# Rows and components of a spectral layer: which queue issues them, and in how many transfers

## The chip, the cores and the metric

The kernel runs on one core of a Trainium2 chip. The core has four compute engines: TensorE (PE, matrix products, its results in PSUM), VectorE (DVE), ScalarE (ACT) and GpSimd (POOL). A fifth, SyncE (SP), only issues transfers (DMAs). SyncE, ScalarE and GpSimd can each issue transfers, in the order of their own instructions; an instruction that waits holds up what stands behind it on its engine. The metric is the device time of one execution in microseconds, as the median over several runs.

## The reference

The input x has 2048 tokens of 1024 channels, in bf16. Four residual layers follow each other, A, B, A, B, each on the layer-normalised input:

```python
def _layernorm(x, axis=-1, eps=1e-5):
    return (x - mean) / jnp.sqrt(var + eps)

def _A_ref(x, w_r, w_i):                       # spectral layer
    X = rfft2(x, axes=(-2, -1))                # over tokens and channels
    X = X * (w_r + 1j * w_i)                   # filter, 2048 x 513
    return irfft2(X, s=(S, D))

def _B_ref(x, w1, b1, w2):                     # 1024 -> 3584 -> 1024
    h = x @ w1 + b1
    return (h * tanh(softplus(h))) @ w2        # mish

x = x + _A_ref(_layernorm(x), A_w_r, A_w_i)
x = x + _B_ref(_layernorm(x), B_w1, B_b1, B_w2)
x = x + _A_ref(_layernorm(x), A_w_r, A_w_i)
x = x + _B_ref(_layernorm(x), B_w1, B_b1, B_w2)
```

## The kernel before, in words

**Order of work.** The program writes the instructions of every engine out by hand. `Prog` holds one engine's instructions; `op`, `group` and `dma` (L200 to L255) derive the waits from what each instruction reads and writes (`Res`). `dma` places a transfer in the queue of the engine that it is given, at the place that the program has reached for that engine. A `Res` that is written by several transfers as `parts` is ready when all of them have landed.

**The prologue** (L382 to L417). SyncE loads x once by tokens into XS (12 transfers, one more from ScalarE), two small tables, and then x a second time in another order, "rows", into XR: partition 8*n2+h, with the 128 positions n1 and 128 channels l along the free dimension. Each transfer of rows moves one h (of 8) and one quarter q of the n1 positions (32 of 128): 16 x 32 runs of 256 bytes, 128 KB. There are 4 x 8 = 32 of them, on three queues:

- quarters 0 and 2: all eight from SyncE;
- quarter 1: even h from SyncE, odd h from GpSimd, whose issue waits until quarter 0 has landed (`reads=self.r_xr[:1]`);
- quarter 3: even h from SyncE, odd h from ScalarE, issued later (`late_rows`, L413 and L596), after ScalarE's square root in `first_scales`.

Behind the rows SyncE issues FD (the tables of the second stage), JT, the first filter rows (`load_w`, L678), the tables FT and BT and the constants.

**The first stage** (`first_scales`, L586, and `s1`, L626). VectorE and ScalarE compute the layer norm's statistics from XS. A table of scales is transposed on TensorE (L601) and copied (L603). `scaled(j)` (L611) makes the matrices MN for group j from it: on ScalarE for j = 1 (L616, eight small instructions), on GpSimd for j = 2, 4, 9, 10, 11, 13, on VectorE otherwise (L622). Group j of `s1` (16 groups of 8 matmuls, L641) multiplies the rows of positions 8j to 8j+7 with them, so groups 0 to 3 read quarter 0 of XR, 4 to 7 quarter 1, and so on. The result goes to a pair of PSUM banks; three pairs are used in turn here. A copy to Y frees the pair: on ScalarE (L647), on VectorE (L649) for j = 5, 10, 14.

**The other stages** (`order_A`, L1013). Eight groups of components go through s2 (L748, needs Y and FD), s3, the filter (L805 to L837), i1 and i2; `filter_bins` (L1029) prepares a group's filter from rows that were loaded, with four matmuls (L1039) and copies (L1050, L1054). i2 writes group g's components U. `u_turn` (L925) stores them to a scratch tensor in memory, and `u_back` (L949) loads them back in another order into UT, 512 KB in 256-byte runs. Group g's store is followed on SyncE by the load of group g-1. At the end of the layer the order is: i2 of group 6 (copies on ScalarE, L923), `u_turn(6, 1)`, which issues the load of group 5 and then the store of group 6, both from SyncE; then i1 and i2 of group 7, with copies on VectorE (L583) and ScalarE (L579) and its two half stores from ScalarE; `u_back(6)` on SyncE; and `u_last` (L955), four loads of 128 KB for group 7, two from ScalarE and two from SyncE, which wait for both half stores.

**The end of the layer** (L1003 to L1005, L1072). TensorE runs `spin` (4 matmuls, L658), `residual_first` (8, L1067) and `hold` (16 in the first spectral layer, 11 in the second, L663) while the last components travel; then `i4` (L1078) reads UT and the residual is added. The dense layers B follow (L1164), with long streams of matmuls (L1267, L1366).

The second spectral layer (li = 1) takes its rows from layer B through `xn_d` (L545) and `open_xr`, not through the prologue.

Of the kernel before, what the change touches and what calls it, by code (L numbers as in the profile page):

```python
# [7 lines left out]
P = 128  # L8
# [172 lines left out]
class KB:  # L181
# [200 lines left out]
    def prologue(self):  # L382
        sp = self.sp
        self.op(self.pool, lambda e: e.memset(self.EPS[:], 1e-5), writes=[self.r_eps, self.r_warm])
        xt = self.x[0].rearrange("(t p) d -> p t d", p=P)

        for a, b in ((10, 11), (0, 1), (1, 2), (11, 12), (2, 3), (3, 4), (12, 13), (4, 6), (13, 14), (6, 8), (14, 15), (8, 10), (15, 16)):
            self.dma(self.act if a == 10 else sp, self.XS[:, a:b, :], xt[:, a:b, :], f"x{a}", writes=self.r_xs[a:b])
        self.warm(ACT.Sqrt)
        small = {}  # L390
        def load_small(name, n, d):
            b = self.alloc(name, self.o[name], [n], d)
            self.dma(sp, b.ap, self.con[name], name.lower(), writes=[b.res])
            small[name] = b
        load_small("M0", P, BF)
        load_small("IDF", P, F32)
        self.M0, self.IDF = small["M0"], small["IDF"]

        self.XR = self.alloc("XR", self.o["XR"], [P, P])
        self.r_xr = []  # L400
        xv = self.x[0].rearrange("(n2 n1) (h l) -> h n2 n1 l", n2=16, l=P)
        self.r_xr = [Res(f"xr{q}") for q in range(4)]

        def rows(q, h, prog):
            self.dma(prog, self.XR.ap[h:P:8, 32 * q:32 * q + 32, :], xv[h][:, 32 * q:32 * q + 32, :], f"xr{q}{prog.name}",
                     parts=[self.r_xr[q]], reads=self.r_xr[:1] if prog is self.pool else [])
        for q in range(4):
            for h in range(8):
                if h % 2 == 0 or q not in (1, 3):
                    rows(q, h, sp)  # L410
                elif q == 1:
                    rows(q, h, self.pool)
        self.late_rows = lambda: [rows(3, h, self.act) for h in (1, 3, 5, 7)]  # L413
        self.dma(sp, self.FD[:], self.con["FD"], "fd", writes=[self.r_fd])
        load_small("JT", 4 * P, BF)
        self.JT, self.r_jt = small["JT"].ap, small["JT"].res
        self.w1_next = 0  # L417
# [168 lines left out]
    def first_scales(self):  # L586


        dve, act = self.dve, self.act
        for j in range(10):  # L590
            self.stats_dve(j)
        for j in range(10, 16):
            self.stats_act(j)
        self.sums_to_mv(10, 6)
        self.root(0, 16)
        self.late_rows()  # L596
        rt = self.alloc("RT", self.o["RT"], [16, 8], F32)
        self.op(dve, lambda e: e.tensor_copy(rt.ap, self.RS[:, 2, :].unsqueeze(2).to_broadcast([P, 16, 8])),
                reads=self.r_rs, writes=[rt.res])
        bank = self.r_bank[7]  # L600
        self.group([lambda e: e.transpose(self.PS[:, 7, 0:P], rt.ap.rearrange("p a b -> p (a b)"), self.IDF.ap)],  # L601
                   reads=[rt.res, self.IDF.res], writes=[bank])
        self.op(dve, lambda e: e.tensor_copy(rt.ap.rearrange("p a b -> p (a b)"), self.PS[:, 7, 0:P]), reads=[bank], writes=[rt.res])  # L603
        self.MN = self.alloc("MN", self.o["MN"], [P, P])
        self.r_mn = [Res(f"mn{j}") for j in range(16)]
        for r in self.r_mn:
            r.inherit(self.MN.res)
            r.begin()
        self.RT = rt
# [108 lines left out]
    def layer_A(self, li):  # L718
# [7 lines left out]
        dve, act, sp, pool = self.dve, self.act, self.sp, self.pool  # L726
# [198 lines left out]
        def u_turn(g, half):  # L925

            u = U[g % 3]
            if g == 7:
                h = slice(8 * half, 8 * half + 8)
                if half == 0:  # L930
                    u_back(6)
                self.dma(act, self.u_d[g][:, h, :], u.ap[:, h, :], f"uwh{half}", reads=[u.res], writes=[self.r_ud7[half]])
                if half:
                    u_last()
            elif half:
                if g == 6:
                    u_back(5)
                self.dma(sp, self.u_d[g], u.ap, f"uw{g % 3}", reads=[u.res], writes=[self.r_ud[g]])
                if 0 < g < 6:
                    u_back(g - 1)  # L940

# [7 lines left out]
        def u_back(g):  # L949
            if self.UT is None:  # L950
                open_ut()
            self.dma(sp, self.UT.ap[g:P:8, :, :], self.u_d[g].rearrange("l r n -> r l n"), f"usp{g % 3}",
                     reads=[self.r_ud[g]], parts=self.r_ut)

        def u_last():  # L955

            for q in range(4):
                l = slice(32 * q, 32 * q + 32)
                self.dma((act, act, sp, sp)[q], self.UT.ap[7:P:8, l, :], self.u_d[7][l, :, :].rearrange("l r n -> r l n"),
                         f"ul{q}", reads=self.r_ud7, parts=self.r_ut[q:q + 1])  # L960
# [17 lines left out]
        for stage, g, h in self.order_A():  # L978
            if stage == 2:
                s2(g, h)  # L980
                if li == 0 and h == (g < 2):
                    filter_bins(g)
                    if g in (0, 1):
                        load_w(g + 5)
                    elif g == 4:
                        load_w(7)
            elif stage == 3:
                s3(g, h)
                if h:
                    if 1 <= g < 6:  # L990
                        load_tabs(g + 2)
                    if li == 0:
                        self.keep_filter(g)
                    elif g < 4:
                        load_w(g + 4)
            elif stage == 4:
                i1(g, h)
                if h and g < 6:
                    load_btabs(g + 2)
            else:  # L1000
                i2(g, h)
                u_turn(g, h)
# [817 lines left out]
```

## Time and profile before

| what | value |
|---|---|
| median of 6 runs | 928.25 us (925.96 to 930.62) |
| profiled execution | 928.99 us |
| its span, first to last instruction | 927.2 us |
| TensorE busy | 880.7 us (95%) |
| VectorE, ScalarE, GpSimd busy | 623.6, 435.2, 150.0 us |
| transfers | 175.99 MB, mean 190 GB/s |
| first matmul of the first stage (L641) | 22.61 us |
| first matmul of the second stage (L748) | 39.89 us |
| `i4` starts (L1078), first and second spectral layer | 112.70 and 560.85 us |

The profiled execution lies 1.8 us above its span and 0.7 us above the median of the runs. In the timeline a row gives start, duration, engine, line, operation and tiles, how many instructions are merged, and in brackets how long the engine stood idle before it and what ended the wait. An engine's name with a q (SPq, ACTq) is its queue: issuing a transfer, which is not counted as busy. In the chain of work that ended last, each piece is what the next one waited for; "issue" is time for which the profile shows no reason. L251 is the line of the helper `dma`, so all transfers carry it.

### The profile page before, as it was taken

Reading aid. Unit: us, or ns where it says so; the run is one execution under the profiler, and the core shown is the slowest. Engines: PE = TensorE matmul, PEld = TensorE weight load, DVE = VectorE, ACT = ScalarE, POOL = GpSimd, SP = SyncE. Lnnn points to the kernel's source line nnn. Section 1 sums busy time; section 2 is a strip of 40 time slices with the busy share of each in tenths; the row PEclk is TensorE's granted clock in tenths of the full one; section 3 lists DMA queues with packets and bytes.
Section 4 is the critical chain, followed back from the end, with each engine's and each line's share of the span. In section 5 each row is a group of like instructions: output and inputs, shape, how many; then the busy total and the mean of one; then the engine's idle time right before and its main releaser. Section 6 shows DMA issues by size and latency. Waiting matters only on the chain.

```text
span 927.2 us, 13620 instructions
## 1 busy us (share of the span) xinstructions
PE 880.7 (95%) x5503; PEld 473.4 (51%) x5503; DVE 623.6 (67%) x995; ACT 435.2 (47%) x645; POOL 150.0 (16%) x174
## 2 busy tenths in 40 slices
PE   0899989999999999999998998999999999999998
PEld 0677576444444444444446766754444444444443
DVE  7698468687789667568767765666747655554473
ACT  7899485456213485420018975757550015552000
POOL 1732003960004651010121200000000000000000
PEclk9999999999999999999999999999999999999999
DMA  9979872674786388364732786445165545732442
GB/s 275 272 251 273 224 190 67 215 279 120 279 272 240 132 323 292 123 233 142 279 92 104 227 220 152 145 160 173 46 194 189 194 141 191 275 120 83 174 121 110
DMA packets 151711, 175.99 MB, mean 190 GB/s; under 512 B 73080, under 2 KB 130648, under 8 KB 151528
## 3 DMA queue, kind: packets, MB, share of 16 engines
q1 hardware_dynamic: 136160, 129.27, 45.1%
q0 software_dynamic: 10224, 43.42, 12.8%
q10 hardware_dynamic: 5264, 2.43, 1.1%
q8 instruction: 43, 0.70, 0.3%
q14 instruction: 20, 0.16, 0.1%
HBM read 130.78 MB, written 40.89 MB: 185 GB/s over the span
## 4 chain that ended last, share of the span: by engine, by line
PE 87%; DVE 6%; ACT 5%; DMA 1%; issue 1%; ACTq 0%; SPq 0%; DVEq 0%
PE PS L1366 37%; PE PS L1267 30%; PE PS L1227 6%; PE PS L748 3%; PE PS L849 2%; ACT ARENA L457 2%; PE PS L879 2%; PE PS L1078 2%; PE PS L641 1%; PE PS L1188 1%; PE PS L911 1%; PE PS L1067 1%; PE PS L663 1%; ACT ARENA L647 1%; DVE ARENA L1193 1%
## 5 line engine op out<-in xcount | busy, mean ns | idle before, releaser
L1366 PE MATMUL PS<-ARENA 128*128 128x512 bf16 x1568 | 340.1, 379 | 0.0
L1267 PE MATMUL PS<-ARENA 128*128 128x512 bf16 (+1 forms) x1288 | 280.3, 379 | 0.8 <-DVE ARENA L1272 0.8
L1366 PEld LDWEIGHTS PS<-ARENA 128*128 128x128 bf16 x1568 | 153.3, 98 | 184.5
L1272 DVE TENSOR_TENSOR ARENA<-PS,ARENA 128x512 f32<-128x512 f32 x230 | 157.1, 691 | 100.0 <-PE PS L1267 92.2
L1267 PEld LDWEIGHTS PS<-ARENA 128*128 128x128 bf16 x1288 | 125.4, 98 | 153.2 <-DVE ARENA L1272 3.5
L1277 ACT ACTIVATE ARENA<-ARENA,B 128x512 bf16<-128x512 f32 x138 | 98.8, 721 | 69.1 <-DVE ARENA L1272 63.7
L579 ACT ACTIVATE ARENA<-PS 128x512 f32<-128x512 f32 (+3 forms) x86 | 61.6, 726 | 110.8 <-PE PS L1267 92.4
L1160 POOL TENSOR_TENSOR ARENA<-ARENA 128x512 bf16<-128x512 bf16 x56 | 71.4, 1275 | 74.7 <-DVE ARENA L528 61.1
L457 ACT ACTIVATE ARENA<-XS 128x1024 bf16<-128x1024 bf16 x60 | 63.2, 1053 | 36.4 <-DVE XS L1417 33.1
L1227 PE MATMUL PS<-ARENA 128*128 128x256 bf16 (+1 forms) x528 | 74.8, 299 | 3.4 <-DVE ARENA L1193 1.9
L1391 DVE TENSOR_TENSOR ARENA<-ARENA 128x3584 bf16<-128x3584 bf16 x32 | 63.9, 2017 | 0.0
L1227 PEld LDWEIGHTS PS<-ARENA 128*128 128x128 bf16 x528 | 50.8, 99 | 22.9 <-DVE ARENA L1193 3.3
L1417 DVE TENSOR_TENSOR XS<-PS,ARENA 128x512 bf16<-128x512 f32 x52 | 35.7, 690 | 39.0 <-PE PS L1366 38.7
L1409 DVE TENSOR_TENSOR ARENA<-PS,ARENA 128x512 f32<-128x512 f32 x48 | 32.9, 688 | 27.7 <-PE PS L1366 27.3
L1231 ACT ACTIVATE ARENA<-PS,B 128x256 bf16<-128x256 f32 (+1 forms) x66 | 33.2, 515 | 30.2 <-PE PS L1227 30.0
L1277 ACT ACTIVATE ARENA<-PS,B 128x512 bf16<-128x512 f32 x46 | 31.5, 685 | 18.4 <-PE PS L1267 18.4
L1405 DVE TENSOR_TENSOR ARENA<-ARENA,XS 128x512 f32<-128x512 f32 x52 | 36.9, 734 | 0.6
L448 ACT ACTIVATE RS<-MV,EPS 128x1 f32<-128x1 f32 (+2 forms) x11 | 3.3, 296 | 71.6 <-DVE MV L570 70.1
L748 PE MATMUL PS<-FD,ARENA 128*128 128x256 bf16 (+1 forms) x256 | 31.4, 271 | 2.5 <-ACT ARENA L647 1.3
L849 PE MATMUL PS<-ARENA 128*128 128x256 bf16 x256 | 32.6, 273 | 1.0 <-DVE ARENA L814 0.6
L805 ACT ACTIVATE ARENA<-PS 128x1024 bf16<-128x1024 f32 x30 | 30.4, 1046 | 5.0 <-PE PS L796 5.0
L1242 DVE TENSOR_TENSOR ARENA<-ARENA 128x2048 f16<-128x2048 bf16 x16 | 25.3, 1582 | 9.0 <-PE PS L1227 8.7
(103 smaller groups left out, 817.7 us busy)
## 6 DMA issues: line engine op xcount, KB each, us to landing
ARENA<-in_B_w_dram SPq DMA_DIRECT2D x30, 896.0 KB, 6.7
ARENA<-w1s_scratch SPq DMA_DIRECT2D x28, 896.0 KB, 4.8
ARENA<-w2s_scratch SPq DMA_DIRECT2D x24, 896.0 KB, 6.4
w1s_scratch<-ARENA POOLq DMA_DIRECT2D x14, 896.0 KB, 4.5
ARENA<-in_B_w_dram SPq DMA_DIRECT2D x24, 512.0 KB, 4.4
u_scratch<-ARENA SPq DMA_DIRECT2D x14, 512.0 KB, 4.7
ARENA<-u_scratch SPq DMA_DIRECT2D x14, 512.0 KB, 5.8
w2s_scratch<-ARENA POOLq DMA_DIRECT2D x8, 896.0 KB, 4.2
```

What stands on the lines that cost most here:

```text
L457: self.op(act, lambda e, i=i, f=f: e.activation(junk.ap, x, f, accum_out=sums[:, i:i + 1]), reads=[self.r_xs[j]], writes=[junk.res], parts ...
L579: fn = (lambda e: e.activation(dst, src, ACT.Copy)) if scale is None else \
L748: fns.append(lambda e: e.matmul(dst, at(r), FD[:, t:t + n], start=start, stop=stop))
L849: fns.append(lambda e, c=c, part=part: e.matmul(ps[:, c * 256:(c + 1) * 256], yk.ap[:, part, c * P:(c + 1) * P], t[:, (128, 0)[part]:(384, ...
L1160: self.op(self.pool, lambda e, dst=A(dst), x=A(x), y=A(y), op=op: e.tensor_tensor(dst, x, y, op), reads=[b.res] + list(after), writes=[b.rs])
L1227: fns.append(lambda e, db=db, bank=bank, fl=fl: e.matmul(PS[:, bank, 0:w], wb.ap[:, db, fl * P:(fl + 1) * P], x.ap[:, db, tok], start=(db ...
L1267: self.group([lambda e, db=db: e.matmul(PS[:, bank, :], A[:, db, :], mov[:, db, :], start=(start and db == 0), stop=(db == 3), skip_group_ ...
L1272: self.op(dve, lambda e: e.tensor_tensor(dst.ap, PS[:, bank, :], x.ap, ALU.add), reads=[self.r_bank[bank], x.res], writes=[dst.res])
L1277: self.op(act, lambda e: e.activation(at, src, ACT.Mish, bias=self.B1[:, ft:ft + 1]), reads=[res, self.r_b1], writes=[ra])
L1366: self.group([lambda e, i=i, k=k, b=PB[n][k].ap: e.matmul(PS[:, bank, :], ap[:, i, t * P:(t + 1) * P], b[:, i - 7 * k, :], start=(start an ...
L1391: self.op(dve, lambda e: e.tensor_tensor(ap[dst][:, f, :], ap[x][:, f, :], ap[y][:, f, :], op), reads=part(x, k) + part(y, k), writes=part ...
L1405: self.op(dve, lambda e: e.tensor_tensor(a[t], a[t], x, ALU.add), reads=[rx], writes=[r[t]])
```

## The change

Two edits.

1. The rows are loaded in 24 transfers, all from SyncE: quarters 0 and 1 together in eight transfers of 256 KB, which share one `Res`, then quarters 2 and 3 in eight each of 128 KB. GpSimd and ScalarE issue none; `late_rows` and its call go.
2. `u_turn` issues the store of group 6's components from ScalarE's queue, not SyncE's, in both spectral layers. The load of group 5, ahead of it in the program, stays with SyncE.

```diff
@@ prologue
-        self.r_xr = [Res(f"xr{q}") for q in range(4)]
-
-        def rows(q, h, prog):
-            self.dma(prog, self.XR.ap[h:P:8, 32 * q:32 * q + 32, :], xv[h][:, 32 * q:32 * q + 32, :], f"xr{q}{prog.name}",
-                     parts=[self.r_xr[q]], reads=self.r_xr[:1] if prog is self.pool else [])
-        for q in range(4):
+        for q, n in ((0, 2), (2, 1), (3, 1)):
+            r = Res(f"xr{q}")
             for h in range(8):
-                if h % 2 == 0 or q not in (1, 3):
-                    rows(q, h, sp)
-                elif q == 1:
-                    rows(q, h, self.pool)
-        self.late_rows = lambda: [rows(3, h, self.act) for h in (1, 3, 5, 7)]
+                s = slice(32 * q, 32 * (q + n))
+                self.dma(sp, self.XR.ap[h:P:8, s, :], xv[h][:, s, :], f"xr{q}", parts=[r])
+            self.r_xr += [r] * n
@@ first_scales
         self.root(0, 16)
-        self.late_rows()
@@ u_turn
                 if g == 6:
                     u_back(5)
-                self.dma(sp, self.u_d[g], u.ap, f"uw{g % 3}", reads=[u.res], writes=[self.r_ud[g]])
+                self.dma(act if g == 6 else sp, self.u_d[g], u.ap, f"uw{g % 3}", reads=[u.res], writes=[self.r_ud[g]])
```

## The prediction

> **What bounds the kernel now.** I read the chain that ended last first, then its pieces in order of time around both edited places, then the timeline, the row transfers and the busy time by stretch. Over the whole span of 927.2 us the chain is TensorE:
>
> ```profile
> PE 87%; DVE 6%; ACT 5%; DMA 1%; issue 1%; ACTq 0%; SPq 0%; DVEq 0%
> ```
>
> So what the edits touch is a small part, and each matters only where the chain leaves TensorE's steady stream. The first place is the prologue. Its pieces (start us, us, what):
>
> ```profile
> 19.86 0.36 ACTq L251
> ...
> 21.61 0.65 ACTq L251
> ...
> 22.36 2.45 ACT ARENA L616 x8
> 24.82 0.05 issue
> 24.86 2.74 PE PS L641 x24
> 27.60 0.95 issue
> 28.55 5.99 PE PS L641 x56
> ...
> 34.57 1.23 DVE ARENA L649
> 35.80 2.26 DVE ARENA L622 x2
> 38.06 1.14 DVE ARENA L649
> 39.20 0.69 issue
> 39.89 1.69 PE PS L748 x16
> ```
>
> ScalarE's four row issues (L251) stand on the chain ahead of the scaled matrices of group 1 (L616); groups 1 to 3 of the first stage follow (L641). Then comes a hole of 0.95 us with no engine named. Group 4 starts there, the first that reads the second quarter of the rows; half of that quarter is issued by GpSimd. The second stage begins at 39.89 when the copy of group 15 is done (38.77 plus 1.02 us on ScalarE). The timeline (start, us, engine):
>
> ```profile
> 8.11 22.82 SPq L251 DMA_DIRECT2D ARENA<-in_A_x_dram  x24
> ...
> 19.57 2.66 POOL L251 DMA_DIRECT2D ARENA<-in_A_x_dram  x4 [18.72 <-DMA ARENA<-in_A_x_dram]
> ```
>
> GpSimd waits for the first quarter, so that quarter has landed at 19.57. Its own four issues start at 19.57 to 21.61; the median of them lands 5.7 us after its start, so the last at 27.3 or, with the delay of a loaded queue, later: I read the hole's end at 28.5 as this landing. The issue times by transfer (ns min/median/max), rows and then the components' loads, which have the same 256-byte runs but four times the bytes (512 KB against 128 KB):
>
> ```profile
> L251 SPq DMA_DIRECT2D ARENA<-in_A_x_dram x24: 627/628/3087, 8.1 to 30.3; - x24
> ...
> L251 SPq DMA_DIRECT2D ARENA<-u_scratch x9: 532/538/1640, 68.1 to 109.8; - x9
> ```
>
> An issue costs 0.53 to 0.63 us whatever its size, when the queue has room. The stretches (us, PE, PEld, DVE, ACT, POOL, clock, DMA share, GB/s):
>
> ```profile
> 15.00:21.00 6.00, 0.48 (x1) 0.18 (x1) 4.23 (x13) 4.06 (x9) 1.43 (x3) 1.00 0.97 198
> 21.00:28.00 7.00, 3.75 (x32) 3.25 (x32) 6.95 (x7) 5.42 (x12) 6.90 (x7) 1.00 1.15 232
> 28.00:32.00 4.00, 3.44 (x33) 3.48 (x34) 1.66 (x3) 2.50 (x3) 4.00 (x3) 1.00 1.23 217
> ```
>
> From 15 to 21 us one 131 KB issue every 0.67 us gives 195 GB/s: SyncE's pace, not the engines'. With a backlog the rows reach 232 (three queues) or 217 GB/s (SyncE almost alone).
>
> The second place is the end of each spectral layer. In the first layer:
>
> ```profile
> 100.03 0.60 ACT L579 ACTIVATE ARENA<-PS 128x512 bf16<-128x512 f32 x1
> ...
> 100.23 1.45 SPq L251 DMA_DIRECT2D u_scratch<-ARENA  x1
> ...
> 101.23 0.60 ACT L579 ACTIVATE ARENA<-PS 128x512 bf16<-128x512 f32 x1 [0.60 <-PE PS L849]
> ...
> 109.06 3.66 PE L663 MATMUL PS<-BD,ARENA 128*128 128x512 bf16 x16
> ...
> 112.70 0.95 PE L1078 MATMUL PS<-MT,ARENA 128*128 128x32 bf16 x32
> ```
>
> TensorE fills the wait for the components with 16 filler matmuls (L663, 16 x 216 ns, so to 112.5), and the reads start at 112.70.
>
> **The Trainium skill.** "DMA: Bandwidth & Descriptors", section Issuing engines are not separate DMA queues: transfers of all issuers run on the same 16 DMA engines, and several issuers save issue time alone. The trace agrees in kind: three queues give 232 GB/s, one with a backlog 217. The same page, Queues, rings and completion order: the engines alternate between queues packet by packet; so GpSimd's and ScalarE's rows share bandwidth with SyncE's third quarter from 21 us. "TensorE: Matmul & The Clock Gate", Part 1: the array runs at half clock until one free-running window of about 3.4 us is busy, so a hole can delay the full clock. In the trace, first-stage matmuls start 107 ns apart to 34.2 us and 55 ns apart after it, 5.6 us after the hole.
>
> **The change, part by part.**
>
> *SyncE's rows.* 8 + 4 + 8 + 4 = 24 issues become 8 + 8 + 8 = 24; eight carry 256 KB. By the loads of 512 KB the larger ones cost no more to issue (0.63 us), so 24 x 0.63 stays; what waits behind them (FD, JT, the first filter rows) is held by the same 4 MB, and I move it by 0 to 0.7 us. The fourth issue's 3.09 us shows a full queue; larger transfers meet it sooner, but it then has work.
>
> *When the first half lands.* The first quarter is at 19.57 now. The second follows it directly, 1.05 MB: at 198 GB/s 5.3 us, so 24.9; at 217, 4.8 us, and the first gains 0.3, so 24.1; at 232, 23.6; at the 280 GB/s of the stretch 95 to 97 us, 22.4. The larger transfers lift the issue limit; I take 24.0 and keep 22.4 to 24.9.
>
> *ScalarE.* Four issues go, 2.71 us. Its 8 scaled copies wait for VectorE's scales, which end at 21.34, so they start at 21.4, not 22.36, and end at 23.85. *GpSimd.* Four issues go, 2.66 us; its scaled matrices start about 0.95 us earlier and gate nothing.
>
> *The first stage.* Group 0 now waits for both quarters, 24.0, not 22.61: late by 1.4, on nobody's path, as group 1 stands at 24.86. The groups then run back to back at 8 x 107 = 0.853 us: group 4 starts at 24.0 + 4 x 0.853 = 27.4, not 28.55: 1.15 us gained. ScalarE's copies, one per 0.93 us, keep the three PSUM pairs free: copy 0 ends at 26.2, group 3 asks for its pair at 26.6. Group 8 asks for the third quarter near 31 and group 12 for the fourth near 34; at 217 GB/s they land at 28.9 and 33.8. VectorE's steps behind group 10 (1.23 + 2.26 us) shift along. Without the hole the full clock can come up to 3 us sooner; the copies (0.93 against 0.44 us per group) then set the pace, which is worth 0 to 0.7 us; I take 0.3. The second stage starts near 38.4. A cap stands behind it: the filter matmuls at 41.42 need filter rows that land at 39.4 (VectorE waits for them there), so at most 2.0 us pass through. Sum of this part: -1.45 us, bounds -2.0 and, at 24.9, -0.25.
>
> *Group 6's store.* SyncE's 1.45 us issue goes; it stood behind the load of group 5's components. ScalarE gets one issue in each layer, right after the copy that ends at 100.08: 0.33 us by its own stores of group 7 at 103.73, plus 0.05 for the wait. Queued behind it is the copy at 100.03 (0.60 us), now about 100.5 to 101.1; the next starts at 101.23, waiting for TensorE. Cost 0, with 0.13 us in hand; a stall as long as SyncE's 1.45 would cost 1.0 us per layer, but ScalarE's queue is empty then. The store no longer waits behind the 512 KB load and lands up to 2 us sooner; SyncE's next load (105.45) follows. What gains: in layer 0 the reads start 0.2 us after the fillers; in layer 1 directly behind them. So -0.2 and 0; against it, the earlier load runs beside group 7's stores and could delay the last loads by up to 0.5 us where they are just in time. I take -0.1.
>
> **Sum.** -1.45 - 0.1 = -1.55 us on the span of 927.2, so 925.65. The profiled execution took 928.99 (1.8 us outside the span) and becomes 927.45. The median of the runs is 928.25; the same difference gives 926.7. About 0.3% (2.8 us) is the least that a measurement of this kernel can tell from no change, so this counts as none.
>
> **Rivals.** *Capped (B):* the filter rows land 0.7 us later and take the prologue's gain. For it: VectorE waits for them at 39.41. Against: their wait is 0.21 us, and the same bytes stand ahead of them. It gives 927.6 to 928.6.
>
> *Late rows (C), the slower side:* a 256 KB transfer needs twice the room in the queue, SyncE issues the next only when half has drained, and the engines run dry in between. For it: the stalls of 3.09 and 2.15 us. Against: with 512 KB loads queued the engines kept 231 GB/s from 99 to 103 us. At worst each transfer waits for the one ahead: 262 KB in 1.21 us (217 GB/s) plus 0.63 us of issue, 143 GB/s. I allow 1.4 us from last byte to landing (half of the 2.8 us that the shortest row transfer takes in all); then 3.2 us x 198 GB/s = 0.63 MB of the first quarter were left at 15 us, and with the second 1.68 MB. At 143 GB/s they take 11.7 us, the half is there at 28.1, group 4 starts at 31.5, 3.0 us late, and the kernel takes 931.2. The rival decides from 25.15 us on (24.0 plus 1.15, about 200 GB/s); below 145 GB/s it is slower by over 0.3%.
>
> *More (D):* rows at 280 GB/s; group 1 is then bound by ScalarE's 23.85, group 4 starts at 26.4 (-2.1), and with the full clock early and filter rows moved along the gain is 2.3 to 3.3: 925 to 926.
>
> **Chances.** A (-0.7 to -2.3) 0.50, B 0.17, C 0.19, D 0.14. A and B lie within 0.3%; of C I give 0.11 past it, as its rate is unbounded below, and of D 0.09. So faster 0.09, same 0.80, slower 0.11. The range, 924.4 to 930.4, covers A, B, most of D and the milder half of C, with some 0.7 us for the median of six runs (925.96 to 930.62); what is left out is 0.12 above and 0.06 below. A alone has 925.9 to 927.6.
>
> **What would show it.** In the changed profile: SyncE's first eight row issues at about 0.63 us with stalls; no row issue on ScalarE or GpSimd; the first L641 group near 24.0 and no hole before the fifth; L616 from 21.4; L748 near 38.4; L641's 55 ns spacing before 34.2. At the layers' ends: ScalarE's store near 100.1 at 0.33 us, the copy behind TensorE still 0.60 after its matmul, the load of group 6 sooner, L1078 directly behind L663. The forecast is wrong if the first L641 group starts after 25.2, if L748 follows FD or filter rows, or if L1078 stands behind its loads.

## The result, and the profile after

The changed kernel takes 929.94 us (median of 16 runs, 928.27 to 934.75); the kernel before, in all its runs beside it, 927.57 (37 runs). The ratio is 1.0029 with an interval of 1.0018 to 1.0039: slower by 2.7 us (1.7 to 3.6), close to the 0.3% that the prediction took as the least that can be told from no change. It had put the median at 926.7 us and counted that as no change. The profiled executions agree: a span of 929.1 us against 927.2. Below, layer 1 and layer 2 are the first and the second spectral layer.

The chain of waits over the whole span of the changed kernel:

```profile
PE 83%; DVE 6%; DMA 4%; ACT 4%; SPq 2%; issue 1%; ACTq 0%; DVEq 0%
```

Where TensorE held 87% and transfers 1%, TensorE now holds 83% and transfers 4%. The chain therefore leaves TensorE in more places. Its pieces in the prologue (start us, us, what):

```profile
20.07 5.13 DMA ARENA<-in_A_x_dram
...
25.24 1.05 PE PS L634 x8
...
26.31 6.53 ACT ARENA L640 x7
...
38.89 1.69 PE PS L741 x16
40.58 0.45 PE PS L1032 x4
```

The first-stage group (L634, L641 before) waits for the last row transfer of the first half and starts at 25.24. The hole ahead of the fifth group is gone, ScalarE's copies (L640) set the pace, and the second stage (L741) starts at 38.89, 1.0 us sooner than in the profile of before. The stretches over the row loads (us, PE, PEld, DVE, ACT, POOL, clock, DMA share, GB/s) show how fast they came:

```profile
15.00:21.00 6.00, 0.48 (x1) 0.18 (x1) 4.37 (x14) 3.86 (x9) 0.00 (x0) 1.00 1.12 205
21.00:28.00 7.00, 2.76 (x27) 2.76 (x28) 6.93 (x7) 4.13 (x10) 6.77 (x4) 1.00 1.13 215
```

205 GB/s, not much above the 198 of before: larger transfers did not open a faster rate. The ends of the two spectral layers, in the same chain:

```profile
103.79 5.24 DMA u_scratch<-ARENA
...
554.23 4.88 DMA u_scratch<-ARENA
...
559.18 3.13 DMA ARENA<-u_scratch
...
562.45 0.95 PE PS L1071 x32
```

Here the time is lost. In the second layer of before no transfer stood here; the reads (L1078 then, L1071 now) followed the fillers without a gap:

```profile
558.64 2.37 PE PS L663 x11
561.01 0.79 PE PS L1078 x32
```

Now the reads wait for a store of 4.88 us and a load of 3.13 behind it. TensorE's waits in the changed kernel, from 550 to 566 us (idle us, times, longest):

```profile
PE PS L1071 <- DMA ARENA<-u_scratch: 1.4, 1, 1.4
```

From the first filler behind the last components (L651 now, L658 before) to the first read, layer 1 takes 8.69 us (7.91 before) and layer 2 8.21 (6.68). These +0.78 and +1.54 us and some 0.6 lost in the stretches between and after, less the 1.0 gained in the prologue, make up the 1.9 us between the spans.

The store that now lasts 4.88 us is the second half of group 7's components. It issues where it did, and in the kernel before landed 2.12 us after its issue, by the same view:

```profile
DMA to landing us min/median/max: 2.1/2.1/2.1
```

What changed around it is the order of issues. The timeline of before (start, us, engine):

```profile
553.11 0.33 ACTq L251 DMA_DIRECT2D u_scratch<-ARENA  x1
554.17 0.33 ACTq L251 DMA_DIRECT2D u_scratch<-ARENA  x1
555.06 0.53 SPq L251 DMA_DIRECT2D ARENA<-u_scratch  x1
```

and of the changed kernel:

```profile
553.17 0.33 ACTq L251 DMA_DIRECT2D u_scratch<-ARENA  x1
553.41 0.53 SPq L251 DMA_DIRECT2D ARENA<-u_scratch  x1
554.23 0.33 ACTq L251 DMA_DIRECT2D u_scratch<-ARENA  x1
```

SyncE's load of group 6 (512 KB in runs of 256 bytes) waits for the store of group 6. That store lands sooner, so the load goes out at 553.41, ahead of group 7's last store and not behind it. The records of the transfers' packets say the same: the store's first packet moves 2.8 us after its issue (within 0.9 before). From 555.9 to 557.0 us the changed kernel moves packets of SyncE's queue (q1) alone, and none of ScalarE's, whose store was issued at 554.23 (packets, MB, their time as a share of 16 engines' time, each packet counted in full):

```profile
q1 hardware_dynamic: 1156, 0.30, 129.1%
```

About three quarters of the load's packets have started when the store's begin. The four loads of group 7 (`u_last`) wait for it, and the reads for them.

### The profile page after: what moved, and what is told of

Same layout as the page of the kernel before. It is cut to its first block, busy times and chain, and to the rows that moved or that the text cites. A ratio compares the mean times of both kernels' runs of the same rounds, so it can differ in the third digit from the quotient of the medians.

```text
span 929.1 us, 13610 instructions
## 1 busy us (share of the span) xinstructions
PE 878.4 (95%) x5503; PEld 470.7 (51%) x5503; DVE 623.8 (67%) x995; ACT 435.2 (47%) x645; POOL 147.6 (16%) x170
## 4 chain that ended last, share of the span: by engine, by line
PE 83%; DVE 6%; DMA 4%; ACT 4%; SPq 2%; issue 1%; ACTq 0%; DVEq 0%
PE PS L1359 35%; PE PS L1260 30%; PE PS L1220 6%; PE PS L741 3%; PE PS L842 2%; SPq L251 2%; PE PS L872 2%; PE PS L1071 2%; ACT ARENA L640 1%; DMA ARENA<-in_B_w_dram 1%; DMA u_scratch<-ARENA 1%; PE PS L1181 1%; ACT ARENA L451 1%; ACT ARENA L573 1%; DMA ARENA<-u_scratch 1%
## 5 line engine op out<-in xcount | busy, mean ns | idle before, releaser
L1224 ACT ACTIVATE ARENA<-PS,B 128x256 bf16<-128x256 f32 (+1 forms) x66 | 33.2, 515 | 30.3 <-PE PS L1220 30.0
L1270 ACT ACTIVATE ARENA<-PS,B 128x512 bf16<-128x512 f32 x46 | 31.5, 685 | 18.4 <-PE PS L1260 18.4
L741 PE MATMUL PS<-FD,ARENA 128*128 128x256 bf16 (+1 forms) x256 | 31.4, 271 | 2.5 <-ACT ARENA L640 1.3
```

The costliest lines, as they stand in the source:

```text
L741: fns.append(lambda e: e.matmul(dst, at(r), FD[:, t:t + n], start=start, stop=stop))
L1270: self.op(act, lambda e: e.activation(at, src, ACT.Mish, bias=self.B1[:, ft:ft + 1]), reads=[res, self.r_b1], writes=[ra])
```

## The experiments

The theory is that the loss is the store's edit, through the early load ahead of group 7's last store. Against it stand two others: that the loss comes from ScalarE's queue, which carries one more store, or that it comes from the rows' edit and the layers' ends only pass it on. A second question is why the prologue's gain doesn't reach the time. Times are medians, of 14 to 22 runs where an interval is given; a ratio is to the kernel before on the same chips.

**Each edit alone.** The rows' edit alone:

```diff
-                self.dma(act if g == 6 else sp, self.u_d[g], u.ap, f"uw{g % 3}", reads=[u.res], writes=[self.r_ud[g]])
+                self.dma(sp, self.u_d[g], u.ap, f"uw{g % 3}", reads=[u.res], writes=[self.r_ud[g]])
```

> The rows' edit alone; group 6's store stays with SyncE. Both theories on the layers' ends (load ahead, shared queue; see the next run) put the loss in the store's edit: the second stage then starts near 38.9 us as in the changed kernel (39.89 before), both layers' ends are as before (i4 about 0.2 us behind the fillers in the first layer, directly behind them in the second), and the time is 1.0 us under the kernel before (0.9989). If the rows cost the time, for instance through what follows them in SyncE's queue, it is over the kernel before by up to 2.5 us.

The kernel before with the store's edit alone:

```diff
-                self.dma(sp, self.u_d[g], u.ap, f"uw{g % 3}", reads=[u.res], writes=[self.r_ud[g]])
+                self.dma(act if g == 6 else sp, self.u_d[g], u.ap, f"uw{g % 3}", reads=[u.res], writes=[self.r_ud[g]])
```

> The store's edit alone; rows as before. Theory load ahead: SyncE, free of the store, issues the load of group 6 about 2 us sooner, ahead of group 7's second half store, and this store lands about 5 us after its issue (2.1 in the second layer before). Theory shared queue: group 6's store stands in ScalarE's queue ahead of group 7's. Both expect i4 0.8 to 1.0 us later in the first layer and 1.5 us later in the second, so 2.3 to 3.5 us over the kernel before (1.0025 to 1.004). If the store's edit costs nothing, the time is that of before.

Rows alone: 928.15 us, ratio 1.0009 (0.9995 to 1.0023), span 927.1. Store alone: 930.37, 1.0029 (1.0019 to 1.0040), span 928.9. The store's edit carries the whole loss; the rows' edit makes no difference that can be told, and the gain of 1.0 us expected of it is missing. The chain of the store alone, end of layer 2 (start us, us, what):

```profile
554.29 4.76 DMA u_scratch<-ARENA
...
559.12 3.35 DMA ARENA<-u_scratch
...
562.61 0.95 PE PS L1078 x32
```

The store of 4.76 us and the load behind it stand there as in the changed kernel, without any change of the rows.

**The same order from SyncE, ScalarE's queue untouched.** In the kernel before, SyncE issues the store of group 6 ahead of the load of group 5:

```diff
+                self.dma(sp, self.u_d[g], u.ap, f"uw{g % 3}", reads=[u.res], writes=[self.r_ud[g]])
                 if g == 6:
                     u_back(5)
-                self.dma(sp, self.u_d[g], u.ap, f"uw{g % 3}", reads=[u.res], writes=[self.r_ud[g]])
```

> The kernel before with two transfers of SyncE exchanged at the end of each spectral layer: group 6's store is issued ahead of the load of group 5, not behind it. ScalarE's queue is as before. The store lands about 2 us sooner and so the load of group 6 starts sooner, near 103.4 us. Theory load ahead: group 7's second half store lands about 5 us after its issue and the time is 2 to 3.5 us over the kernel before. Theory shared queue: nothing of ScalarE's has changed, so the time is that of before within 0.5 us.

931.17 us, ratio 1.0036 (1.0026 to 1.0046). Its timeline and then its chain:

```profile
553.82 0.53 SPq L251 DMA_DIRECT2D ARENA<-u_scratch  x1
...
555.08 0.33 ACTq L251 DMA_DIRECT2D u_scratch<-ARENA  x1
```

```profile
555.08 5.38 DMA u_scratch<-ARENA
...
560.53 3.24 DMA ARENA<-u_scratch
...
563.91 0.95 PE PS L1078 x32
```

The load of group 6 again goes out ahead of the last store, which lands after 5.38 us. ScalarE issues here exactly what it did before, so that theory falls: what matters is when group 6's store lands and what it releases.

**The load put back behind the store.** Two kernels keep both edits and move only the load of group 6. In the first, SyncE issues it once all of group 7's components are written:

```diff
@@ u_turn, g == 7
-                if half == 0:
-                    u_back(6)
...
                 if half:
+                    u_back(6, sp, [u.res])
                     u_last()
@@
-        def u_back(g):
+        def u_back(g, prog=sp, after=()):
...
-            self.dma(sp, self.UT.ap[g:P:8, :, :], self.u_d[g].rearrange("l r n -> r l n"), f"usp{g % 3}",
-                     reads=[self.r_ud[g]], parts=self.r_ut)
+            self.dma(prog, self.UT.ap[g:P:8, :, :], self.u_d[g].rearrange("l r n -> r l n"), f"usp{g % 3 if prog is sp else 'a'}",
+                     reads=[self.r_ud[g]] + list(after), parts=self.r_ut)
```

> The changed kernel, with one wait more: SyncE issues the load of group 6 when group 7's components are all written, so at about the moment of group 7's second half store, not 0.4 to 0.8 us before it. Group 6's store stays in ScalarE's queue. Theory load ahead: that half store lands 2.1 to 3.5 us after its issue, i4 stands directly behind the fillers in both layers, and the time is 3 us under the changed kernel, 1.0 under the kernel before. Theory shared queue: the half store lands as late as in the changed kernel, near 5 us, and the time stays near 930.

In the second, the added line is `u_back(6, act)`, directly behind group 7's last store on ScalarE:

> The changed kernel, with the load of group 6 issued by ScalarE right behind group 7's second half store, so 0.35 us after it and in the same queue. Theory load ahead: the half store lands 2.1 to 2.5 us after its issue in the second layer (4.88 in the changed kernel), the last loads start by 556.5, i4 is directly behind the fillers, 6.7 us after the first of them (8.21 in the changed kernel), and the time is 2 to 3 us under the changed kernel. If group 6's store in the same queue were what counts, the half store would still need near 5 us.

927.86 us, ratio 1.0005 (0.9992 to 1.0017), and 927.95 us, 1.0001 (0.9990 to 1.0013): the loss is gone in both. The timeline of the second and its chain:

```profile
552.17 0.33 ACTq L251 DMA_DIRECT2D u_scratch<-ARENA  x1
...
552.53 0.59 ACTq L251 DMA_DIRECT2D ARENA<-u_scratch  x1
```

```profile
552.17 2.60 DMA u_scratch<-ARENA
...
554.84 4.25 DMA ARENA<-u_scratch
...
559.22 0.95 PE PS L1070 x32
```

With the load 0.36 us behind it the store lands after 2.60 us. The last loads now stand behind the load of group 6 and take 4.25 us, not 3.13, but store and loads together are 1.2 us shorter (6.9 against 8.1), and the reads start 7.05 us after the first filler (8.21). In the first of the two the load is issued 0.02 us ahead of the store, the store lands after 2.77 us, and the reads start after 7.32. So the harm comes somewhere between 0.02 us ahead and the changed kernel's 0.82.

Over all profiles of the study the split is clean. Where the load of group 6 goes out ahead (changed kernel twice, store alone, SyncE's order), layer 2's last store takes 4.76 to 5.38 us and the reads start 8.21 to 8.84 us after the fillers; in the thirteen others without an added load 2.02 to 2.83 and 6.45 to 7.72. In layer 1 the reads start after 8.51 to 9.99 us against 7.56 to 8.43, so the groups nearly touch. The store itself is less clear there: 4.94 to 6.23 us with the load ahead, but 2.37 to 4.68 with it behind, 4.37 in the kernel before; what holds it up in those isn't known. Against the medians of the thirteen the changed kernel's two profiles lose 0.75 and 1.5 us at the two ends, which is most of its 2.7.

**Bytes or small runs?** The load ahead moves 512 KB in runs of 256 bytes. To ask which of the two delays the store, the last load stays behind the store on ScalarE, and a further load of the same 512 KB, in 128 runs of 4 KB, goes out early from SyncE. It fills the buffer that the components came from, which nothing reads afterwards; it adds that one transfer per layer.

```diff
@@ u_turn, g == 7, with u_back(6, act) behind the last store
+                if half == 0:
+                    self.dma(sp, U[0].ap, self.u_d[6], "ucoarse", reads=[self.r_ud[6]], writes=[U[0].res])
```

> The changed kernel with the load of group 6 behind the last half store (as in the run before that did so), and at its early place on SyncE another load of the same 512 KB, in 128 runs of 4 KB into group 6's own buffer. It adds 512 KB of loads in each layer. If bytes ahead hold up the store, its second half lands 1.4 us later than with no load there (2.60 us from issue to landing in the second layer), so at 3.5 to 4.2 us. If it is the number of 256-byte pieces ahead, it lands at 2.6 to 3.0 us.

The timeline of this kernel has the extra load 1.03 us ahead of the last store:

```profile
555.48 0.33 SPq L251 DMA_DIRECT2D ARENA<-u_scratch  x1
...
556.51 0.33 ACTq L251 DMA_DIRECT2D u_scratch<-ARENA  x1
```

A single run took 931.24 us. In layer 2 the store landed after 3.82 us, between 2.60 and 4.88; in layer 1 after 6.19, against 4.48 without the extra load and 5.24 in the changed kernel. So 512 KB in long runs ahead delay the store too: in layer 2 by about half as much as small runs do, in layer 1 by more. Small runs are not needed for the delay, and what they add is not settled by one run. An estimate: at the 231 GB/s that the kernel before moved from 99 to 103 us, with such loads queued, 512 KB take 2.3 us, and 2.60 + 2.3 = 4.9 is what the store took in the changed kernel's layer 2. That the store simply stands behind all that was issued ahead of it fits. Whether it waits at the transfer engines or already where the two queues' transfers are cut into packets stays open.

A third kernel sent the load of group 6 from GpSimd, at its old place, to see whether another issuer takes the delay away:

```diff
                 if half == 0:
-                    u_back(6)
+                    u_back(6, pool)
```

> The changed kernel, with the load of group 6 issued by GpSimd in place of SyncE, at the same early place. It separates two ways in which the load can hold up the store. If its bytes do it (the engines are shared), the half store in the second layer still lands near 5 us after its issue and the time is as in the changed kernel, near 930. If it is that SyncE's 2048 descriptors go through what makes ScalarE's descriptors too, GpSimd's own descriptors stay out of the way: the store's packets start about 0.9 us after its issue, it lands in 2.1 to 3.5 us, and the time is 1.5 to 2.5 us under the changed kernel.

928.44 us, 1.0001 (0.9983 to 1.0018), and the last store landed after 2.83 us. But this doesn't tell the theories apart. The timeline has the issue ahead of the store (552.30):

```profile
551.57 1.08 POOL L251 DMA_DIRECT2D ARENA<-u_scratch  x1 [21.19 <-DMA u_scratch<-ARENA]
```

while the load's first packets move at 554.23 only, when nine tenths of the packets of group 7's two half stores have started. GpSimd's load was late enough to restore the order by itself.

**Why the prologue's gain isn't seen.** The prediction took the hole of 0.95 us and the late full clock from one profile. Here are two more profiles of the kernel before and one of the changed kernel, both unchanged:

> The kernel before, unchanged, profiled once more. Theory clock: the hole ahead of group 4 (0.95 us) and the clock that came up only at 34.3 us belong to the one execution that was profiled, not to the kernel; here the clock comes up at 27.5 to 31.5, the first filter matmul starts at 39.4 to 39.9 us, not at 41.42. Theory hole: the hole and the late start are the kernel's own, 28.5 and 41.4 again.

> The same once more, with the same two forecasts: first filter matmul at 39.4 to 39.9 us (clock) or at 41.4 (hole).

> The changed kernel, unchanged, profiled once more. By the other five profiles with its rows the first filter matmul starts at 39.9 to 40.5 us, and the second half store of group 7 lands 4.5 to 5.5 us after its issue in both layers, with i4 8.2 to 9.2 us behind the first filler.

The chains of before, first and second repeat:

```profile
27.88 0.94 issue
28.82 5.57 PE PS L641 x56
...
39.73 1.69 PE PS L748 x16
```

```profile
31.10 1.07 PE PS L641 x16
...
38.17 1.69 PE PS L748 x16
```

These runs took 927.24, 928.16 and, for the changed kernel, 930.3 us. The first repeat has the hole and a second stage at 39.7, as in the profile shown ahead of the prediction; the second has a hole of 0.3 us only, and its second stage starts 1.6 us sooner. With the two kernels that keep the rows of before, its prologue has been seen five times: first filter matmul at 41.42, 41.27, 39.70, 39.47 and 39.87 us. The prediction had one of the two late ones.

In all five, group 4 starts 0.1 us after the last of GpSimd's rows lands (28.46 and 28.55 in the profile of before), so the hole was read rightly. But the hole alone doesn't make a prologue late. In the kernel with SyncE's order (start us, us, engine; idle time in brackets):

```profile
28.51 1.50 PE L641 MATMUL PS<-ARENA 128*128 128x128 bf16 x24 [0.96 <-issue]
```

Here the matmuls behind the hole start 55 ns apart at once, and the second stage starts at 38.30. The late start goes with the full clock: it comes at 34.3 and 33.7 us in the two late profiles and at 28.5 to 29.7 in the three others. In five profiles this is a correlation; no run here shows it as the cause.

With all rows on SyncE in 256 KB transfers seven profiles give 39.87 to 41.44 us for the first filter matmul, median 40.39, against a median of 39.87. The latest is the changed kernel's repeat, forecast at 39.9 to 40.5: its second stage itself waits for FD, to 38.90, and from 39.5 runs at half clock. The two sets overlap; by the medians the rows' edit loses some 0.5 us in the prologue, and a gain of 1.45 isn't there. The place is in the chain of the rows' edit alone:

```profile
24.45 6.11 PE PS L634 x56
...
33.62 6.79 DMA ARENA<-in_A_w_i_dram
...
40.46 0.63 PE PS L1032 x4
```

The first stage runs without a hole, but the first filter matmuls (L1032) now wait for filter rows that SyncE issues at 33.6. In the five profiles with the old rows they start 1.53 to 1.57 us behind the second stage, with nothing between; with the new rows 1.53 to 2.54, median 1.96. One queue for all rows issues FD, and what follows it, later: at 31.7 to 32.5, against 30.3 to 31.5, 0.9 us by the medians.

Two kernels were to test the other half of the reading, the clock, by holding it up. Matmuls that nobody reads run through the two waits of the prologue, in the kernel before (12 at the second place) and in the rows' edit alone (40 there):

```diff
+        def fill(n):
+            self.group([lambda e: e.matmul(self.PS[:, 6, 0:P], self.M0.ap, self.M0.ap, start=True, stop=True)] * n,
+                       reads=[self.M0.res], writes=[self.r_bank[6]])
+        fill(50)
...
+        fill(12)
```

> The kernel before, with TensorE kept busy by matmuls whose result nobody reads: 50 before the table of scales is transposed and 12 behind it, so that the clock is up when the first stage begins. Theory clock: where the second stage starts with the rows of before (39.89, 37.94 and 38.30 us in three profiles) hangs on the moment at which the array's clock comes up (34.3, 29.2 and 28.5 us), so here it starts at 37.5 to 38.0 us, and the median is 0.5 to 1.0 us under the kernel before. Theory rows: the start is set by the GpSimd and ScalarE issues and stays at 38 to 40 us.

> The rows' edit alone, with 50 and 40 such matmuls, so that the clock is up until the first half has landed (24.5 to 25.2 us). Theory clock: with it up in both kernels the rows' edit is worth nothing; the groups run at 0.93 us each, by the copies, from 24.5 on, group 4 starts at 27.5 to 28.0 and the second stage at 37.5 to 38.3, within 0.4 us of the kernel before with the clock up. Theory rows: the edit gains the 1.0 us of the two first profiles here too, so the second stage starts 1 us ahead of the other kernel with the clock up.

926.65 us, ratio 0.9992 (0.9976 to 1.0007), and 928.38 us, 1.0008 (0.9996 to 1.0021). No gain can be told. But the first doesn't test what it was meant to, as the clock was not held. The stretch from the end of group 0 has a granted clock of 0.50 (us, PE, PEld, DVE, ACT, POOL, clock, DMA share, GB/s):

```profile
22.90:29.60 6.70, 4.78 (x47) 4.70 (x46) 5.17 (x6) 6.48 (x12) 6.70 (x5) 0.50 1.25 227
```

The full clock is back at 29.6 us, and the second stage starts at 38.00, like the three early profiles without such matmuls. In the second kernel the clock holds to 34.7 us, and still the second stage starts at 39.44, not at 37.5 to 38.3. Its chain:

```profile
24.93 9.28 ACT ARENA L645 x10
...
34.38 7.24 DMA ARENA<-in_A_w_i_dram
...
41.66 0.63 PE PS L1037 x4
```

The first stage reaches group 12 before its rows (it goes on at 34.71, at half clock to 38.1), and the filter rows land at 41.6, 2.2 us after the second stage has started. In this profile the filter rows set when the filter matmuls start, whatever the clock did ahead of them.

Does the size of the transfers matter? All rows on SyncE in 32 pieces of 128 KB, with the same waits:

```diff
-                s = slice(32 * q, 32 * (q + n))
-                self.dma(sp, self.XR.ap[h:P:8, s, :], xv[h][:, s, :], f"xr{q}", parts=[r])
+                for k in range(q, q + n):
+                    s = slice(32 * k, 32 * k + 32)
+                    self.dma(sp, self.XR.ap[h:P:8, s, :], xv[h][:, s, :], f"xr{q}", parts=[r])
```

> The rows' edit alone with all 32 pieces of 128 KB from SyncE, same waits: the size of the transfers by itself. If SyncE's issue time sets the pace (0.67 us for 131 KB, 195 GB/s), the first half lands at 25 to 26 us (24.3 to 25.2 with 256 KB) and FD goes out about 3 us later, near 35; if the transfer engines do, both are as with 256 KB.

A single run took 929.44 us. The first half lands at 24.58 (24.1 to 25.2 with 256 KB): the size of the transfers did not set its landing. FD goes out at 32.78 and the first filter matmul starts at 42.01, the latest of all; one profile doesn't say whether that is the pieces' doing.

If late filter rows take the gain, giving ScalarE back its four late row transfers should return it. The rows' edit alone, but the odd transfers of the last quarter issued as before:

```diff
+                if q < 3 or h % 2 == 0:
+                    self.dma(sp, self.XR.ap[h:P:8, s, :], xv[h][:, s, :], f"xr{q}", parts=[r])
...
+        self.late_rows = lambda: [self.dma(self.act, self.XR.ap[h:P:8, 96:128, :], xv[h][:, 96:128, :], "xr3a", parts=[r])
+                                  for h in (1, 3, 5, 7)]
@@ first_scales, behind self.root(0, 16)
+        self.late_rows()
```

> The rows' edit alone, with one part of it undone: the odd h of the last quarter again from ScalarE behind its square root. SyncE issues 20 row transfers, not 24. Theory tail of SyncE's queue: in the rows' edit FD goes out at 31.7 to 32.6 us (30.1 to 31.1 with the rows of before), the filter rows behind it arrive later, and the first filter matmul waits for them at about 40.4; here FD goes out at 29 to 30, that matmul starts at 39.3 to 39.7, and the time is 0.5 to 1 us under the rows' edit. If the first stage itself (group 0 at 24.5 us) sets it, the matmul stays at 40.4 and the time at 928.

> The rows' edit with the odd h of the last quarter from ScalarE, once more, to see whether it beats the kernel before. By its first measurement 0.9989 of it, 1 us; if the pair of measurements together does not hold it clear of 1, it is not told from the kernel before.

And the same with the 50 and 40 matmuls that nobody reads:

> The same with TensorE kept busy by 50 and 40 matmuls that nobody reads, so that the clock is up. Theory tail: with neither the clock nor the filter rows late, group 4 starts near 27.0 as in the rows' edit with the clock up, the first filter matmul at 38.5 to 39.3, and the time is 1 us under the kernel before (0.999). The groups' copies at 0.93 us each allow no more than that. If it stays at 40 us or above, something else in the row order holds it.

The first kernel: 926.39 us, 0.9989 (0.9975 to 1.0003), and in the second measurement 927.39, 0.9996 (0.9982 to 1.0011). In its two profiles FD goes out at 30.61 and 30.40 us (forecast 29 to 30) and the first filter matmul starts at 40.02 and 39.72 (forecast 39.3 to 39.7), 1.53 us behind the second stage in both. So the wait for filter rows is gone, as the theory has it; but two of the seven profiles with all rows on SyncE show 1.53 as well, and the time isn't told from that of the kernel before.

With the added matmuls: 927.34, 0.9996 (0.9985 to 1.0007). The first filter matmul starts at 40.74, not at 38.5 to 39.3. The clock is up through the first stage, but it falls again at 37.7, and the second stage's first 16 matmuls, 1.69 us elsewhere, take 3.15 in the chain:

```profile
37.80 3.15 PE PS L750 x16
```

No kernel of the study beats the kernel before with any certainty.

## Why the prediction was wrong, point by point

*Group 6's store* is the step that failed. It named the mechanism in one clause ("the earlier load runs beside group 7's stores and could delay the last loads by up to 0.5 us"), gave it a bound without a working, and took -0.1 us. The measured cost is 2.7 us in the times, of the changed kernel (1.7 to 3.6) and of the store's edit alone (1.8 to 3.7), and +0.78 and +1.54 us at the two layers' ends in the profiles. Two things were missed. First, the order: SyncE's load was put down to the first layer's 105.45, "sooner", without asking where it lands against ScalarE's last store. In the second layer of before that store was issued 0.89 us ahead of the load, and a release 2 us sooner must turn the two around. Second, the size: by the prediction's own 231 GB/s a load of 512 KB takes some 2.3 us, an estimate that would have been a bound; the store lost 2.8 us in layer 2, of which the reads felt 1.5. That the reads stood directly behind the fillers was seen (in layer 1 too, where the 0.2 us taken as a gap is the end of the last filler in the view), and it meant that there was next to no slack; it was used to say that nothing could be gained, not that all that is late is lost. What the step said of ScalarE was right: the issue takes 0.33 us (99.12), the copy behind it goes out at 99.50, and the next still starts 0.02 us after its matmul, at 100.24.

*SyncE's rows.* The count was right, the pace wasn't. 24 issues of 0.63 us were kept, but SyncE was held up: on the chain the issues ahead of the last row transfer of the first half take 3.62, 1.44, 1.15, 1.17 and 1.06 us. FD was moved by "0 to 0.7 us"; it went from 30.97 to 32.47, 1.5 us.

*When the first half lands.* Forecast 24.0 (22.4 to 24.9). By the start of group 0 it is 25.24 in the changed kernel and 25.15 in its repeat, outside the bounds, and 24.1 to 24.6 in the nine other profiles with 256 KB transfers, inside them; why the two are later isn't known. But "the larger transfers lift the issue limit" was wrong: the rate was 205 GB/s, and 128 KB pieces land their half as early.

*ScalarE and GpSimd.* As forecast: no row issue on either, scaled matrices from 21.18 and 21.23 us that gate nothing.

*The first stage.* Within the two profiles the forecast is nearly met: second stage at 38.89 (near 38.4), no hole, full clock at 28.8 and not 34.3. But -1.45 us was taken from a profile that stood at the late end of the kernel's own spread. This is the second term that failed: against the median prologue of before nothing is left, and the rows' edit alone measures 1.0009, so between 0.5 us gained and 2.1 lost. The gain of 1.0 us between the two profiles was luck. The step's cap was right in kind: the filter rows do come later and take what is gained. That is rival B, capped, and it fits the rows' part.

*Rivals and signs.* Of the prediction's signs of being wrong, two came: the first group at 25.24 us, just past 25.2, and the reads behind their loads; in the repeat the second stage follows FD, a third. Late rows (C) had its deciding point at 25.15 us, where the changed kernel lies, but the rows' edit isn't what made it slower. The sign came from a mechanism that no rival carried, and so the chance of slower, 0.11, was too low.

## What to carry to other kernels

Before releasing a transfer sooner, list what it releases in turn and lay those issues beside the small transfer that ends the stage: here a load with slack that went out 0.8 us ahead of a store without slack delayed it by 2.8 us, and the reads behind it by 1.5. A gain read from a hole in one profile is worth what a second profile of the same kernel leaves of it.

## What the runs showed of the hardware

- In layer 2 a 512 KB load of 256-byte runs on one queue, issued 0.8 to 1.3 us ahead of a store on another, raised the store's time to landing from 2.0 to 2.8 us to 4.8 to 5.4 us. In layer 1 the ranges are 2.4 to 4.7 and 4.9 to 6.2 us. The Trainium skill ("DMA: Bandwidth & Descriptors", Queues, rings and completion order) has the engines alternate between queues packet by packet, by which one expects the store to get a share early; in the changed kernel the store's first packet moved 2.8 us after its issue, with three quarters of the load's packets started, so such sharing is seen over the load's last quarter only. No run shows why.
- The prologue of one kernel came in two forms 1.6 us apart, the full clock starting anywhere from 28.5 to 34.3 us in the profiles of before and of the kernels with its rows. "TensorE: Matmul & The Clock Gate", Part 1, says that the clock's window is free-running and that the point of change varies by 0.5 us either way from run to run; the starts here lie 5.8 us apart, far more than that, and no run set the window's phase.
- GpSimd's load of 512 KB moved its first packets 2.3 us (layer 1) and 2.7 us (layer 2) after its issue; ScalarE's last store of before moved its own within 0.9 us.
- In the changed kernel's repeat the granted clock fell to 0.50 from 39.5 to 42.9 us, behind a wait of 1.3 us for FD ahead of the second stage; in the kernel before a wait of 1.2 us there left it at 1.00.
